# mLSTM cell and leaky-ReLU feed-forward: cells in fewer groups, k, v and x asked for by ScalarE, and three float32r products in groups 4 and 5

## The chip, the cores and the metric

The kernel runs on one core of a Trainium2 chip. Times are device microseconds (us) of one execution. Shown for the kernel before are the median of three runs, 513.25 us (510.64 to 513.26), and one profiled execution. PE is TensorE, PEld its weight loads, DVE VectorE, ACT ScalarE, POOL GpSimd, SP SyncE.

## The reference

An mLSTM cell runs over a sequence; its output, rearranged to one row of 320 values per token, passes a two-layer feed-forward with a leaky ReLU:

```python
batch, n_heads, seq, head_dim = (4, 8, 768, 40)          # d_model 320, d_ff 2048
for t in range(S):
    m_new = np.maximum(f_gate[:, :, t] + m, i_gate[:, :, t])
    f_stab = np.exp(f_gate[:, :, t] + m - m_new)
    i_stab = np.exp(i_gate[:, :, t] - m_new)
    C = f_stab[:, :, None, None] * C + i_stab[:, :, None, None] * np.einsum('bhd,bhe->bhde', vt, kt)
    n = f_stab[:, :, None] * n + i_stab[:, :, None] * kt
    h_tilde = np.einsum('bhde,bhe->bhd', C, qt)
    denom = np.maximum(np.abs(np.einsum('bhd,bhd->bh', n, qt)[:, :, None]), 1.0)
    y[:, :, t] = h_tilde / denom / (1.0 + np.exp(-o_gate[:, :, t]))
...
x = y.transpose(0, 2, 1, 3).reshape(B * S, H * D)         # 3072 x 320
h = x @ w_in                                              # 320 x 2048
out = np.maximum(0.01 * h, h) @ w_out                     # 2048 x 320
```

All of it is float32 (the two weight matrices arrive as 64-bit words and are made float32 on the chip).

## The kernel before, in words

**Chunks, steps, groups.** The sequence is cut into NB = 6 chunks c of 128 tokens. A cell step s = 4c + b is one chunk of one of the four batches. The four steps of chunk c make x of group c: 512 tokens, on which the feed-forward then works. So cells of a later chunk run beside the feed-forward of an earlier group.

**The first product** of a group (`ff_units`, its matmul on line 759) makes 2048 hidden columns in 16 blocks f of 128, two blocks to a pair j, one on each half of the partitions (row group r). The 320 rows of the contraction are five slots of 64; for each slot there is one matmul per row group, with 64 rows of weights and 512 tokens of x. A pair is two units: three slots, then two slots and two Prelus on ACT (line 767), which take the two PSUM banks `ph` to the tile `acts`. These banks are two of the four in the pool `psf`; the cells have four of their own in `psc`.

**The second product** of groups 1 to 5 (`fast_units`) goes by seven block products in place of eight, each for two batches n: 14 units, in the order p1, p2, p6, p7, p4, p5, p3, each of 16 matmuls of 160 columns (line 835) into one bank of `psf`. Sums on DVE (lines 853, 858, 862, 870, 887, 892; `mix_early`, line 822), copies on ACT (854, 867, 875, 881) and sums on POOL (868, 876, 882) empty these banks or make operands; line 848 sends rows out through SP. Group 0 has a plain second product (line 794). A group of 1 to 5 thus has 30 units: 16 and 14.

**The cells** of chunks 2 to 5 come in pairs of steps. `u_parts` (scores on lines 614 and 619, DVE on 596 and 624) and `u_mix` (matmuls on line 695, transposes on DVE on lines 702 and 713, POOL on 709, four writes of x to DRAM on line 716 by SP) are a step's two units. `ahead(s)` prepares a later step: exponentials on ACT (458), transposed k and q on DVE (505, 511), the state on POOL (592). `prep_mask` (450) is POOL's. `feed` asks for a step's data: `load`, with k on line 356 and four pieces of v on line 359, and `spread`, line 413; `load_blocks` fetches q, k and o in blocks (398), `spread_q` (421) gate rows. `gather_x` (line 730) reads x back from DRAM in the layout of the first product, four DMAs a step. All these DMAs are on SP.

**The order.** PE, DVE, ACT and POOL run in the order in which the program is written (`manual_schedule`); SP's DMAs are placed by the scheduler. A last loop, lines 1043 to 1103, writes the order: for chunk c it goes through the 30 units of group c - 1 and lays chunk c's cell units behind the unit numbers in `place` (chunk 1) or `pairs` (chunks 2 to 5):

```python
pairs = (2, 2, 6, 6, 14, 14, 19, 19, 19)
```

So chunk 5's cells run beside group 4, and group 5 runs alone. In a unit's place come, in order: steps of exponentials, masks at units 0 and 12, the unit itself, cell units, gathers (from unit 15 on, all steps that are mixed), `ahead`, and `feed`.

**Memory.** Cell tiles (k and q operands, S, rb, w, kqT and others) lie in pools that stay open to the end: `consts` and `wk`. DMAs use eight semaphores in turn, whichever engine asks; a DMA waits for the eighth before it.

Of the kernel before, what the change touches and what calls it, by code (L numbers as in the profile page):

```python
# [10 lines left out]
U32 = mybir.dt.uint32  # L11
U64 = mybir.dt.uint64
# [6 lines left out]
def kernel(  # L19
# [58 lines left out]
    dr = ctx.enter_context(tc.tile_pool(name="dr", bufs=1, space=bass.MemoryType.DRAM))  # L78

# [39 lines left out]
    kn = consts.tile([P, NL, H, DP], F32, name="kn")  # L119
    qn = consts.tile([P, NL, H, DP], F32, name="qn")  # L120
    S_t = [consts.tile([P, 2, H, DP], F32, name=f"S{n}") for n in range(NL)]
    S_v = [t[:].rearrange("p u h (k d) -> p u h k d", d=QW) for t in S_t]
    rb_t = [consts.tile([P, 3, RW], F32, name=f"rb{n}") for n in range(NR)]
    xb = consts.tile([P, PR * TB, QW], F32, name="xb")
# [147 lines left out]
    def gates(c):  # L272


        m0 = m0s.get(c)
        n = P if c == 0 else BH
        fc, il = (f0[:], i0[:]) if c == 0 else (fi[c][:, 0, :], fi[c][:, 1, :])
        F = wk.tile([n, P], F32, name="F", bufs=1)
        nc.vector.tensor_tensor_scan(F[:], fc, zeros[:n].to_broadcast([n, P]), 0.0, op0=ALU.add, op1=ALU.add)
        if c > 0:  # L280
            il_t = wk.tile([BH, P], F32, name="il", bufs=1)
            nc.vector.tensor_scalar(il_t[:], il, scalar1=m0[:], scalar2=None, op0=ALU.subtract)
            il = il_t[:]
        m = wk.tile([n, P], F32, name="m", bufs=1)
        nc.vector.tensor_tensor_scan(m[:], fc, il, -1e30 if c == 0 else 0.0, op0=ALU.add, op1=ALU.max)
        a = wk.tile([n, P], F32, name="a", bufs=1)
        nc.vector.tensor_tensor(a[:], F[:], m[:], op=ALU.subtract)
        bu = wk.tile([BH, 3, P], F32, name="bu", bufs=1)
        nc.vector.tensor_tensor(bu[:, 0, :], il[:BH], F[:BH], op=ALU.subtract)
        if c + 1 < NB:  # L290
            m1 = wk.tile([BH, 1], F32, name="m0")
            if c == 0:
                nc.vector.tensor_copy(m1[:], m[:BH, P - 1 :])
            else:
                nc.vector.tensor_tensor(m1[:], m0[:], m[:, P - 1 :], op=ALU.add)
            m0s[c + 1] = m1
        if c > 0:
            na = wk.tile([BH, 1], F32, name="na")
            nc.vector.tensor_tensor(na[:], m[:, SL - 1 : SL], F[:, SL - 1 : SL], op=ALU.subtract)
        bus[c] = bu, a, (na if c > 0 else None)  # L300
# [42 lines left out]

    def load(s):
        c, b = divmod(s, B)
        rows = ts(c, P)
        d = st.setdefault(s, {})
        n = s % NL
        d.update(k=kn[:, n], q=qn[:, n])
        if c == 0:  # L350
            d["va"] = S_t[n][:, 1]
            parts = [(d["k"][:, :, :D], k), (d["q"][:, :, :D], q), (d["va"][:, :, :D], v)]
            for dst, src in parts:
                nc.sync.dma_start(dst, src[b, :, rows, :].rearrange("h p d -> p h d"))
            return
        nc.sync.dma_start(d["k"][:, :, :D], k[b, :, rows, :].rearrange("h p d -> p h d"))
        for u in range(2):
            for i in range(2):
                nc.sync.dma_start(  # L359
                    S_v[n][ts(u, SL), u, :, i, :DB],  # L360
                    v[b, :, c * P + u * SL : c * P + (u + 1) * SL, DB * i : DB * (i + 1)].rearrange("h p d -> p h d"),
                )
# [43 lines left out]
    def spread(s):  # L406

        c, b = divmod(s, B)
        d = st[s]
        w = wk.tile([P, H, P], F32, name="w", bufs=NL)  # L410
        d["w"] = w[:].rearrange("p h t -> p (h t)")[:, : H * SL].rearrange("p (h t) -> p h t", t=SL)
        for u in range(2):
            nc.sync.dma_start(d["w"][ts(u, SL)], a_dr[c, 0, u, b * H : (b + 1) * H, :].partition_broadcast(SL))

    def spread_q(s):

        c, b = divmod(s, B)
        d = st.setdefault(s, {})
        d["ea"] = wk.tile([P, H, SL], F32, name="ea", bufs=EAB)
        for r in range(2):  # L420
            nc.sync.dma_start(
                d["ea"][ts(r, SL)], a_dr[c, 1, 1 - r, b * H : (b + 1) * H, :].partition_broadcast(SL),
            )

    def spread_first(a, s2):
# [12 lines left out]
        for n in range(2):  # L438
            w = st[s2 + n]["w"] = wk.tile([P, H, P], F32, name="w", bufs=NL)
# [20 lines left out]
    def prep_vu(s):  # L460
# [3 lines left out]
        if s < NS:  # L464
            d["vu"] = wk.tile([P, H, 2, V1], F32, name="vu")
# [34 lines left out]
    def prep_kq(s):  # L500

        d = st[s]
        d["kqT"] = wk.tile([P, 2, PR * P], F32, name="kqT")
# [20 lines left out]
    def u_split(s):  # L524

        d = st[s]
        d["kqT"] = wk.tile([P, 2, PR * P], F32, name="kqT")
# [14 lines left out]
    def u_transpose(s):  # L542
        d = st[s]
        d["kqT"] = wk.tile([P, 2, PR * P], F32, name="kqT")
# [92 lines left out]
    def u_values(s):  # L637
# [4 lines left out]
        d["den"] = wk.tile([P, H], F32, name="den")  # L642
        denominators(d["den"][:], pa[:, :, D])

    def gate(s):

        d = st[s]
        d["x"] = wk.tile([P, Dm], F32, name="x")
# [7 lines left out]
    def u_plain(s):  # L656
# [13 lines left out]
        den = wk.tile([P, H], F32, name="den")  # L670
        denominators(den[:], hN[:, :, 0, DB])
        if b < 2:
            d["x"] = wk.tile([P, Dm], F32, name="x")[:]
        else:
            d["x"] = wk.tile([P, H, D1], F32, name="hn")[:].rearrange("p h d -> p (h d)")[:, :Dm]
# [8 lines left out]
    def u_mix(s):  # L684
# [16 lines left out]
        hb = wk.tile([P, PR * TB, QW], F32, name="hb", bufs=1)  # L701
        nc.vector.transpose(hb[:].rearrange("p (j n) d -> p j n d", n=TB), in_blocks(pT[:]))  # L702
        den = wk.tile([P, PR * TB], F32, name="den")
# [8 lines left out]
        xq = wk.tile([P, PR * P], F32, name="x")  # L712
# [6 lines left out]
    def gather_x(s):  # L719

        c, b = divmod(s, B)
        if ("xT", c) not in st:
            st["xT", c] = wk.tile([P, KC, GT], F32, name="xT", bufs=1)
        xT = st["xT", c]
        src = x_dr[s].rearrange("(k p) t -> p k t", p=DP)
        for r in range(2):
            at = 0
            while at < KC:
                k0, n = run_of(r, at)
                nc.sync.dma_start(xT[DP * r : DP * (r + 1), at : at + n, ts(b, P)], src[:, k0 : k0 + 2 * n - 1 : 2, :])  # L730
                at += n

# [20 lines left out]
    def ff_units(g):  # L753
        xT = st["xT", g]
# [59 lines left out]
        return firsts + fast_units(g)  # L814
# [104 lines left out]
    def ahead(s):  # L919

        if s < NS:
            if s < 2 * B:
                u_split(s)
# [98 lines left out]
    with tc.manual_schedule(engines={E.PE, E.DVE, E.Activation, E.Pool}):  # L1022
# [20 lines left out]
        for c in range(1, NB + 1):  # L1043
            if c > 1:
                ffs = ff_units(c - 1)
            cells = cell_units(c) if c < NB else []
            n_ff, n_c = len(ffs), len(cells)
            done = fed = 0
            waiting, after = [], []
            for i in range(n_ff):  # L1050
                if c == 1:
                    run(now, 2 if i < 10 else 3 if i < 14 else 4)
                    for n in fetch.get(i, ()):
                        load_weights(QN + n)
                    if i == 0:
                        prep_mask(B)
                        ahead(B)
                        load_fi(3)
                for s, steps in lazy.items():
                    if s in late and late[s] > 0:  # L1060
                        late[s] -= 1
                    else:
                        run(steps, 3)
                for n in masks.get(i, ()) if 1 < c < NB else ():
                    if c * B + n < NS:
                        prep_mask(c * B + n)
                ffs[i]()
                if c + 1 < NB:
                    if i == (1 if c == 1 else 0):
                        gates(c + 1)  # L1070
                    if c == 2 and i == 0:
                        mixed_weights()
                    if i == (3 if c == 1 else 2):
                        gates_exp(c + 1)
                upto = min(n_c, sum(p <= i for p in (place if c == 1 else pairs)))
                while done < upto:
                    fn, s = cells[done]
                    fn(s)
                    done += 1
                    if fn is u_mix:  # L1080
                        waiting.append(s)
                    if fn is u_plain and s < 2 * B - 1 or fn is u_parts and s == 2 * B - 1:
                        ahead(s + 1)
                    elif fn is u_mix:
                        after.append(s + 2)
                    elif fn is u_plain:
                        prep_mask(s + 2)
                        ahead(s + 2)
                if i >= NF - 1:
                    for s in waiting:  # L1090
                        gather_x(s)
                    waiting.clear()
                if i < NF or i >= NF + 8:
                    for s in after:
                        ahead(s)
                    after.clear()
                while fed < done:
                    fn, s = cells[fed]
                    fed += 1
                    if fn in (u_mix, u_plain):  # L1100
                        load_late(s + NR, 2)
                        if s + NL < NS:
                            feed(s + NL)
# [31 lines left out]
```

## Time and profile before

| | us |
|---|---|
| median of the runs shown (lowest, highest) | 513.25 (510.64, 513.26) |
| span of the profiled execution, first to last instruction (no other time is given for it) | 508.0 |
| PE, DVE, ACT, POOL busy | 492.0, 308.1, 171.5, 137.7 |
| mean granted TensorE clock | 0.983 |
| PE starts groups 1, 2, 3, 4, 5 at | 139.3, 214.1, 289.0, 365.3, 439.7 |
| first product of group 5, 439.7 to | 474.3 |

An engine's busy time says how much work it has, not that it sets the end. That is read from the chain that ended last (from the last instruction back to what released each step), and then, stage by stage, from the idle time of the engine that stands in the chain. A row of a group gives line, engine, operation, `out<-in` tiles, count, busy time and mean time of one, then the idle time just before it and what ended most of it.

### The profile page before, as it was taken

The page shows a single profiled execution, that of the slowest core. Times are in us where ns is not written, and L with a number is a line of the kernel's source. Part 1 is how long each engine was busy: PE and PEld are TensorE (multiplying, and loading weights), DVE is VectorE, ACT ScalarE, POOL GpSimd, SP SyncE. Part 2 cuts the span into 40 slices and gives each one's busy share as a digit, 9 for nine tenths or more (in the row PEclk, how much of TensorE's full clock was granted, in tenths as well). Part 3 has the DMA queues.
Part 4 walks back from the last instruction along what each step waited for, and adds up shares of the span by engine and source line. Part 5 has one row for each costly group of instructions (what it writes and reads, how often), then busy time and mean ns, then how long its engine had stood idle before and what let it go on. Part 6 is the DMA issues. An engine that isn't in the chain of part 4 may idle for free.

```text
span 508.0 us, 12526 instructions
## 1 busy us (share of the span) xinstructions
PE 492.0 (97%) x4981; PEld 366.6 (72%) x4981; DVE 308.1 (61%) x515; ACT 171.5 (34%) x478; POOL 137.7 (27%) x175
## 2 busy tenths in 40 slices
PE   8878999999999999999999999999899999999997
PEld 7766878767655489955589855599755599744797
DVE  4779898899954778635765826764825664101321
ACT  3664864652722510323411323311213411022210
POOL 4243443360402404413104614014612003000020
PEclk9877999999999999999999999999999999999999
DMA  9977687888765551565663566564466212200001
GB/s 116 146 204 154 149 219 185 168 152 175 155 145 87 131 124 46 133 130 144 147 132 92 115 137 170 137 141 97 109 135 177 68 53 62 69 1 1 1 1 52
DMA packets 165290, 59.21 MB, mean 117 GB/s; under 512 B 128816, under 2 KB 156016, under 8 KB 165232
## 3 DMA queue, kind: packets, MB, share of 16 engines
q1 hardware_dynamic: 164848, 58.28, 52.2%
q8 instruction: 39, 0.64, 0.5%
q14 instruction: 19, 0.16, 0.1%
q10 hardware_dynamic: 384, 0.13, 0.1%
HBM read 51.68 MB, written 6.70 MB: 115 GB/s over the span
## 4 chain that ended last, share of the span: by engine, by line
PE 79%; DVE 9%; DMA 3%; ACT 3%; POOL 2%; issue 2%; SPq 2%; ACTq 0%; POOLq 0%; DVEq 0%
PE ph L759 36%; PE po L835 26%; PE po L794 6%; PE pT L695 3%; PE sd L614 3%; SPq L359 1%; PE sd L619 1%; DMA S<-in_v_dram 1%; ACT kqT L540 1%; PE tkq L548 1%; DVE raw L261 1%; DMA rb<-in_q_dram 1%; DMA w<-a_dr 1%; PE pa L641 1%; DVE qn L511 1%
## 5 line engine op out<-in xcount | busy, mean ns | idle before, releaser
L759 PE MATMUL ph<-xT,w_in 64*128 64x512 f32 (+1 forms) x1120 | 216.2, 538 | 2.4 <-DVE y L887 1.4
L759 PEld LDWEIGHTS ph<-xT,w_in 64*128 64x128 f32 x1120 | 108.6, 189 | 95.1 <-issue 86.3
L767 ACT ACTIVATE acts<-ph 128x512 f32<-128x512 f32 (+1 forms) x112 | 53.9, 533 | 179.0 <-PE ph L759 178.9
L835 PEld LDWEIGHTS po<-w_out,acts 128*128 128x128 f32 x640 | 87.3, 190 | 3.8 <-issue 3.8
L835 PE MATMUL po<-w_out,acts 128*128 128x160 f32 x640 | 89.1, 300 | 0.0
L450 POOL TENSOR_TENSOR w<-w,i 128x512 f32<-128x512 f32 x20 | 26.9, 1345 | 117.3 <-DMA w<-a_dr 117.2
L624 DVE TENSOR_TENSOR qn<-w,sd 64x512 f32<-64x512 f32 x40 | 27.4, 684 | 40.2 <-PE sd L619 20.5
L458 ACT ACTIVATE w<-w,gT 128x64 f32<-128x64 f32 (+1 forms) x192 | 50.8, 348 | 2.7 <-POOL w L450 1.7
L592 POOL TENSOR_TENSOR S<-S,f 40x336 f32<-40x336 f32 x36 | 32.0, 889 | 67.3 <-PE pT L695 36.3
L835 PE MATMUL po<-raw,acts 128*128 128x160 f32 x320 | 45.5, 300 | 0.0
L835 PEld LDWEIGHTS po<-raw,acts 128*128 128x128 f32 x320 | 43.9, 190 | 0.3
L794 PE MATMUL po<-w_out,acts 128*128 128x320 f32 x128 | 36.5, 436 | 0.0
L702 DVE STREAM_TRANSPOSE hb<-pT 128x512 f32<-128x512 f32 x16 | 11.5, 717 | 31.0 <-PE pT L695 30.8
L794 PEld LDWEIGHTS po<-w_out,acts 128*128 128x128 f32 x128 | 23.6, 190 | 9.3 <-issue 0.3
L511 DVE TENSOR_TENSOR qn<-kqT,ea 64x512 f32<-64x512 f32 x32 | 28.4, 888 | 1.0
L709 POOL TENSOR_TENSOR xb<-xb,den 128x320 f32<-128x320 f32 x16 | 11.7, 729 | 56.8 <-DVE xb L706 56.6
L596 DVE TENSOR_TENSOR S<-S,sd 40x336 f32<-40x336 f32 x36 | 18.1, 503 | 12.1 <-POOL S L592 11.2
L614 PEld LDWEIGHTS sd<-kqT 40*64 40x64 f32 x640 | 19.9, 135 | 6.1 <-issue 6.1
L822 DVE TENSOR_TENSOR raw<-acts 128x1024 f32<-128x1024 f32 x10 | 11.8, 1222 | 18.3 <-ACT acts L767 18.2
L713 DVE STREAM_TRANSPOSE x<-xb 128x512 f32<-128x512 f32 x16 | 18.2, 1140 | 7.6 <-POOL xb L709 7.6
L835 PE MATMUL po<-raw 128*128 128x160 f32 x160 | 22.5, 299 | 0.0
L835 PEld LDWEIGHTS po<-raw 128*128 128x128 f32 x160 | 22.0, 190 | 0.0
(151 smaller groups left out, 551.8 us busy)
## 6 DMA issues: line engine op xcount, KB each, us to landing
w<-a_dr SPq DMA_DIRECT2D x40, 128.0 KB
rb<-in_k_dram SPq DMA_DIRECT2D x64, 80.0 KB
rb<-in_q_dram SPq DMA_DIRECT2D x64, 80.0 KB
rb<-in_o_gate_dram SPq DMA_DIRECT2D x64, 80.0 KB
ea<-a_dr SPq DMA_DIRECT2D x32, 128.0 KB
kn<-in_k_dram SPq DMA_DIRECT2D x24, 160.0 KB
raw<-in_moe_w_out_dram SPq DMA_DIRECT2D x6, 640.0 KB
S<-in_v_dram SPq DMA_DIRECT2D x80, 40.0 KB
```

The costliest lines, as they stand in the source:

```text
L450: nc.gpsimd.tensor_tensor(w, w, cm2.unsqueeze(1).to_broadcast([P, H, SL]), op=ALU.add)
L458: yield nc.scalar.activation(w[:, h, :], w[:, h, :], AF.Exp, bias=gT[c][:, 0, bh : bh + 1], scale=1.0)
L511: nc.vector.tensor_tensor(mixed(s)[rows, 1 - r], d["kqT"][rows, 1].rearrange("p (h t) -> p h t", t=SL), d["ea"][rows], op=ALU.mult,)
L592: nc.gpsimd.tensor_tensor(new, old, g, op=ALU.mult)
L596: nc.vector.tensor_tensor(new, new, st[s]["dC", u], op=ALU.add)
L614: nc.tensor.matmul(bank[1 - u][toks, h, :], lhsT=kqT[rows, 0, ts(h, SL)], rhs=kqT[rows, 1, ts(h, SL)], start=True, stop=True,)
L624: nc.vector.tensor_tensor(mixed(s)[toks, u], w[toks], bank[1 - u][toks], op=ALU.mult)
L713: nc.vector.transpose(in_blocks(xq[:]), xb[:].rearrange("p (j n) d -> p j n d", n=TB))
L759: nc.tensor.matmul(ph[r][:, cols], lhsT=w_row(r, slot, j), rhs=xT[DP * r : DP * (r + 1), slot, cols], start=(slot == 0), stop=(slot == KC ...
L767: nc.scalar.activation(acts[:, f, cols], ph[r][:, cols], AF.Prelu, alpha=0.01)
L794: nc.tensor.matmul(po[n][:], lhsT=acts[:, f, ts(n, P)], rhs=w_out[:, f, :], start=(f == 0), stop=(f == NF - 1),)
L835: nc.tensor.matmul(bank[:], lhsT=left[:, f, :], rhs=right[:, f, :], start=f == 0, stop=f == KH - 1)
```

## The change

It has three parts.

- **Pace.** Ticks take the place of unit numbers: after i + 1 units of group g, the cells stand at tick (30(g - 1) + i + 1) * 4 // 3. Chunk 2's cells still start with group 1, and chunk 5's end at unit 22 of group 3 (tick ENDS = 109) in place of unit 19 of group 4. Order within a tick is as before. At ENDS the cell pools `cc` and `cw`, into which the cell tiles have moved, are closed, and a pool `kp` takes their memory.
- **Asked for by ScalarE.** From chunk 3 on, `load` makes a generator of five DMAs, which ACT issues from two units later on: one a unit in a first product, two in a second. `gather_x` is issued by ACT too, one step a unit, at least three units after the step's `u_mix`. The queue of SP keeps the rest.
- **Three products.** In groups 4 and 5 (in group 4 without its first two pairs, LEAD = 2) the first product of a slot becomes three with float32r operands: raw by raw and low by low into `ph`, dif by dif into a bank `pe` of `psc`. `low` and `dif` of weights and x are made by `split_w_parts` (masking on DVE, difference on POOL, a sum on DVE, a scaled copy on ACT, for each half of 640 columns) and `split_x` (three on DVE for a batch). `raw` weights are copied within SBUF by SP (`fetch_w_part`). `prepare` runs these steps from ENDS on, three a unit in a first product and two in a second; x of group 5 is split in units 4 to 10 of group 4's second product.

```diff
-                nc.sync.dma_start(xT[DP * r : DP * (r + 1), at : at + n, ts(b, P)], src[:, k0 : k0 + 2 * n - 1 : 2, :])
+                nc.scalar.dma_start(xT[DP * r : DP * (r + 1), at : at + n, ts(b, P)], src[:, k0 : k0 + 2 * n - 1 : 2, :])
...
+        if c < 3:
+            for _ in bring(nc.sync):
+                pass
+        else:
+            later[s] = [bring(nc.scalar), 5, clock[0] + 2]
...
+    EPS = 2.0**-12
+    THREE = (NB - 2, NB - 1)
...
+        def first():
+            t = tmp_part()[:].rearrange("p k t -> p (k t)")
+            held.append(t)
+            top_bits(t, src)
+            nc.gpsimd.tensor_tensor(t, t, src, op=ALU.subtract)
+
+        def second():
+            t = held[0]
+            nc.vector.scalar_tensor_tensor(
+                parts["w", "dif"][n][:, at], in0=t, scalar=1.0 + 1.0 / EPS, in1=src, op0=ALU.mult, op1=ALU.add,
+            )
+            nc.scalar.activation(parts["w", "low"][n][:, at], t, AF.Copy, scale=1.0 / EPS)
...
+            def first():
+                ph.extend(psf.tile([P, GT], F32, name=f"ph{r}", tag="mm") for r in range(2))
+                rows(j, ph, "raw", True, False)
+
+            def second():
+                rows(j, ph, "low", False, True)
+
+            def third():
+                pe.extend(psc.tile([P, GT], F32, name=f"pe{r}", tag="c") for r in range(2))
+                rows(j, pe, "dif", True, True)
+                fs = [acts[:, f_of(r, j), :] for r in range(2)]
+                for r in range(2):
+                    nc.scalar.activation(fs[r], pe[r][:], AF.Copy, scale=-EPS)
+                for r in range(2):
+                    nc.vector.scalar_tensor_tensor(
+                        fs[r], in0=ph[r][:], scalar=1.0 + EPS, in1=fs[r], op0=ALU.mult, op1=ALU.add,
+                    )
+                for r in range(2):
+                    nc.scalar.activation(fs[r], fs[r], AF.Prelu, alpha=0.01)
...
+            for i in range(len(ffs)):
+                at["past"] = i >= len(firsts) - 1
+                upto = min(ENDS + 1, (TICKS * (g - 1) + i + 1) * 4 // 3)
+                for m in range(t, upto):
+                    before_tick(m)
                 ffs[i]()
...
+                for m in range(t, upto):
+                    after_tick(m)
+                gather()
+                if t <= ENDS < upto:
+                    open_parts()
+                    for n in range(QN):
+                        fetch_w_part(n)
+                    todo = split_steps()
+                t = max(t, upto)
+                clock[0] += 1
+                bring_later(1 if i < len(firsts) else 2)
+                prepare(3 if i < len(firsts) else 2)
```

## The prediction

> **What bounds the kernel now.** I read the busy times first, then the chain that ended last, then the engines' busy time by stage. The first lines are from the page; the next from the busy time by stretches, cut at the starts of groups 1, 2, 3, 4 and 5 (columns: stretch, its length, busy time and count of PE, PEld, DVE, ACT, POOL, then the granted clock, DMA share, GB/s).
>
> ```profile
> PE 492.0 (97%) x4981; PEld 366.6 (72%) x4981; DVE 308.1 (61%) x515; ACT 171.5 (34%) x478; POOL 137.7 (27%) x175
> ...
> PE ph L759 36%; PE po L835 26%; PE po L794 6%; PE pT L695 3%; PE sd L614 3%; SPq L359 1%; PE sd L619 1%; DMA S<-in_v_dram 1%; ACT kqT L540 1%; PE tkq L548 1%; DVE raw L261 1%; DMA rb<-in_q_dram 1%; DMA w<-a_dr 1%; PE pa L641 1%; DVE qn L511 1%
> ```
> ```profile
> 139.30:214.10 74.80, 74.80 (x775) 54.15 (x774) 49.35 (x76) 21.45 (x65) 21.27 (x25) 1.00 0.49 109
> 214.10:289.00 74.90, 74.90 (x776) 54.17 (x775) 46.08 (x81) 21.05 (x64) 24.07 (x26) 1.00 0.56 129
> 289.00:365.20 76.20, 74.86 (x775) 54.15 (x774) 46.42 (x78) 21.14 (x64) 23.56 (x26) 1.00 0.58 130
> 365.20:439.70 74.50, 74.44 (x704) 54.03 (x704) 36.74 (x64) 16.26 (x44) 12.17 (x16) 1.00 0.41 100
> 439.70:508.00 68.30, 65.25 (x385) 45.86 (x384) 11.98 (x17) 11.03 (x24) 3.14 (x6) 1.00 0.04 13
> ```
>
> The reader is to see that from 139 us on PE has no idle time but 1.4 us ahead of group 4 and the tail, at full granted clock. So only two things change the time there: matmul work, and new waits of PE. Group 5, without cells, costs 65.2 us: 34.6 for the first product (439.7 to 474.3) and 30.7 for the second; a cell chunk adds 9.6 us of PE to groups 1 to 4.
>
> Two more views carry the prices: PE's and PEld's order of time in a first product, PE's waits, and the DMA issues on SP (min/median/max ns).
>
> ```profile
> 236.66 0.19 PEld L759 LDWEIGHTS ph<-xT,w_in 64*128 64x128 f32 x2 [0.23 <-issue]
> 237.09 0.19 PEld L759 LDWEIGHTS ph<-xT,w_in 64*128 64x128 f32 x2 [0.23 <-issue]
> ```
> ```profile
> PE ph L759 <- DVE y L887: 1.4, 1, 1.4
> ```
> ```profile
> L730 SPq DMA_DIRECT2D xT<-x_dr x64: 573/607/1462, 184.9 to 431.6; - x64
> ```
> ```profile
> L359 SPq DMA_DIRECT2D S<-in_v_dram x80: 595/630/2971, 41.9 to 374.6; - x80
> ```
>
> One float32 product of 512 columns is two instructions on each of two row groups (line 759's row counts 1120: 800 for the 400 products of groups 1 to 5, 320 for the 160 of 256 columns in group 0). The row groups run side by side: two loads appear together every 0.43 us. So a pair of products costs 2 x 0.43; over group 5, 34.6 / 40 = 0.865 us.
>
> **The change part by part.**
>
> *Three float32r products.* Six of eight column pairs in group 4 and all eight in group 5, five slots each: 70 pairs of products lose 0.865 us and get three float32r pairs. No row shows a float32r matmul. Bounds: it is at least the shortest spacing of weight loads, 0.11 us (line 641: sixteen in 1.98 us, the last taking 0.28), and I bound it above by one float32 instruction, 0.428 us. That is 70 x (0.33 - 0.865) = -37 us to 70 x (1.284 - 0.865) = +29 us. I take the middle by ratio, 0.214, half a float32 instruction: the row nearest in kind streams the same 512 columns with a split operand. Three cost 0.642; the gain is 70 x 0.223 = **15.6 us**.
>
> The Trainium skill (FP8 and Floating Point Precision, TensorE Precision Notes) says that true FP32 takes four passes and that reduced-precision FP32 is read as four bytes and truncated. One pass would be an estimated 0.216 us by it, the gain 15.1 us; no run shows it yet.
>
> *Epilogue of a triple.* Per column pair ACT gains two copies (0.59 each, line 767) beside its two Prelus, DVE two sums (0.68, line 564). After a third unit PE's bank is free 0.6 + 0.7 + 0.7 = 2.0 us later; PE takes 15 x 0.214 = 3.2 us for the next triple in the other banks. Hidden; if DVE is over 1.2 us behind, it shows.
>
> *Splitting the weights and x.* Per half of 640 columns: DVE 0.49 (line 253) + 0.83 (257), ACT 0.79 (247), POOL 1.1 to 1.6 (from 0.53 at 160 and 0.73 at 320 columns, and from 1.27 at 512 in line 450); I take 1.3, near the first. A batch of x: 0.49 + 0.83 + 0.83 = 2.15 us of DVE. In total 16 x 1.32 + 8 x 2.15 = 38 us of DVE. Group 5's x hides under group 4's second product (DVE busy 12 us in a group without cells). The rest is queued on DVE right behind the last cells, in units 22 to 29 of group 3, and there it is not hidden. Queue it by hand, with t = 0 where PE ends the last cell product. In the trace before, DVE ended that cell's transpose 6.6 us after such an end (417.9 to 424.5). The first masking operation must wait until both last cells' x are in DRAM, since its tile takes their memory: four issues of 0.34 us on SP and 1.4 us to land (from the semaphore times around 164 us): t = 9.7. From there, in program order: three maskings and three differences, waiting for POOL and ACT, to 15.4; x of batch 0 to 17.5; the sums that free bank 1 (the former line 887) 18.1; batch 1 and a masking 20.8; sums freeing bank 2 at 21.4; a difference and batch 2 at 24.3; line 892's sum 24.6; batch 3, a masking, the other sum at 27.6. PE meanwhile: seven units of 2.24 us. The third-last product waits for an ACT copy that stands behind the first new ACT operation: 12.9 in place of 11.2. Group 4's first pair wants both banks: 21.4 in place of 15.7. Its second pair wants the last sum: 27.7 to 32.0, against 24.3 without waits. **7.7 us**, plus 1 for DVE operations that stretch beside POOL (line 511: median 0.73, max 1.54); the 1.4 us of today is in it. Net +7.3. By the time of the first triple, 32 us, every part it needs is made.
>
> *Cells at 4/3.* PE's sum is unchanged; groups 1 to 3 become 65.2 + 4/3 x 9.6 = 78 us. DVE: 12 for the products + 4/3 x 35 = 59 of 78. Enough on average. Where its queue shows: in group 1 the second cell pair's operands (6.0 us in the trace) stand ahead of the second p2 sum, which frees a bank: +1.2 us by the same queue. At unit 27 of group 1 a cell pair and the next pair's operands (7.0 + 6.0 us) stand ahead of the last sums, so group 2's second and third column pair take the banks that the Prelu just before gives back: 1.3 + 0.7 = +2.0 us. Groups 2 and 3 end otherwise: 0.
>
> *Loads asked for by ACT.* 60 loads of k and v (0.43 and 0.63 us) and 64 gathers (0.61): 72 us leave SP's queue and enter ACT's, over 235 us in which ACT is 28% busy; with cells at 4/3 it comes to some 50 of 78 us in a group. What stands behind an issue on ACT are exponentials, Prelus and copies that free banks. A Prelu pair is due 4.3 us after its products and takes 1.2, so 3.1 us of delay cost nothing. I cost it at 0; below zero it can't be, as PE was not idle for SP. It brings one more wait: eight semaphores are shared by both queues, and every DMA waits for the eighth before it in program order, whichever engine asked.
>
> Sum: -15.6 + 7.3 + 1.2 + 2.0 = -5.1 us. The span of 508.0 becomes 502.9. The median shown is 513.25, 5.25 above that span (the lowest run is 2.6 above); I keep the 5.25: **508 us**.
>
> **Rivals.**
> - *The seams are covered*: DVE reaches the parts earlier or banks fall otherwise. For: group ends today cost 0, 0 and 1.4. Then 513.25 - 15.6 + 0 to 5 = 498 to 503.
> - *ACT waits behind SP* (slower). SP waited 29.8 us for DVE at the x writes (line 716), longest 8.6. If an ACT load inherits such a wait by the shared semaphores once in groups 1, 2 and 3, each costs 8.6 - 3.1 = 5.5 us: 508 + 16.5 = 524.5. It decides where ACT stands over 3.1 us in a first product. Against: the loads are delayed by two units, so by over 4 us.
> - *float32r runs at a float32 instruction's pace* (the change doesn't do what it says): 508 + 15.6 + 29 = 553.
> - *Weight loads come out of hiding*: if a load could not run under a matmul of its own row group, a float32r product cost 0.214 + 0.113 = 0.327, three 0.98: +8.1 in place of -15.6, 532 us. The trace speaks against: float32 instructions start 0.43 us apart with 0.19 of load inside.
>
> The Trainium skill (TensorE: Matmul & The Clock Gate, Part 3) says that loads overlap running matmuls only where the row group differs; by that float32 would already show 0.113 more, which the trace does not.
>
> - *In between*: float32r near 0.24 us, or a few more waits: 511 to 516.
>
> **How the numbers follow.** Forecast (503 to 512.5) 0.45; covered seams 0.20; in between 0.07; ACT 0.17; exposed loads 0.04; slow float32r 0.07. 0.5%, about what a measurement of this kernel can tell from no change, is 2.6 us: faster is below 510.7. Of the forecast's 0.45 some 0.35 lie there and 0.10 within. Faster 0.55; same 0.10 + 0.07 + 0.01 = 0.18; slower 0.27. The range reaches from the covered seams to ACT's rival, 497 to 525, and leaves the last two out.
>
> **What would show it.** float32r rows of line 839 of the changed kernel: starts 0.21 us apart for a pair (right), 0.33 or 0.43 (wrong). The first product of group 5 near 26 us in place of 34.6. PE's waits: the first float32 pairs of group 4 on DVE, 6 to 9 us together; about 2 on ACT early in group 2. ACT's waits on DMA over 3 us in groups 1 to 3 would make it wrong, as would PE idle within the triples.

## The result and the profile after

The changed kernel takes 546.57 us (544.56 to 547.68, four runs), the kernel before 511.94 us (509.50 to 513.26) in the same comparison: ratio 1.069, 95% interval 1.064 to 1.073. It is slower, by 35 us, and outside the range that was given. Its profiled execution took 547.39 us with a span of 545.6. One execution of the kernel at 6/5 below took 708 us at a granted clock of 0.65 and is left out of its time.

The page of the changed kernel, engines and chain of work:

```profile
PE 495.0 (91%) x5121; PEld 390.7 (72%) x5121; DVE 361.3 (66%) x583; ACT 194.6 (36%) x514; POOL 154.4 (28%) x183
...
PE 55%; DMA 11%; DVE 11%; SPq 10%; issue 3%; POOL 3%; ACTq 3%; ACT 3%; DVEq 0%; POOLq 0%
```

PE has gone from 97% to 91% of a longer span, and from 79% to 55% of the chain; the chain now runs through DMAs, DVE and SP's queue. Busy time by stretches, cut at the starts of groups 1 to 5 of the changed kernel (columns as before):

```profile
140.30:224.73 84.43, 79.99 (x967) 58.05 (x966) 58.48 (x105) 25.70 (x83) 27.02 (x30) 1.00 0.58 123
224.73:333.64 108.91, 84.31 (x973) 62.95 (x972) 60.91 (x107) 23.26 (x70) 30.02 (x34) 0.91 0.64 145
333.64:414.94 81.30, 76.61 (x707) 55.42 (x705) 56.33 (x85) 22.78 (x64) 27.89 (x27) 0.97 0.43 107
414.94:483.92 68.98, 64.86 (x446) 53.63 (x446) 45.77 (x61) 21.15 (x40) 11.44 (x10) 0.95 0.12 37
483.92:545.60 61.68, 58.51 (x465) 52.83 (x464) 22.10 (x33) 20.76 (x40) 3.13 (x6) 1.00 0.04 14
```

| us | before | after | difference | PE's waits, before and after |
|---|---|---|---|---|
| to the start of group 1 | 139.3 | 140.3 | +1.0 | |
| group 1 | 74.8 | 84.4 | +9.6 | 0 and 4.4 |
| group 2 | 74.9 | 108.9 | +34.0 | 0 and 24.6 |
| group 3 | 76.3 | 81.3 | +5.0 | 1.4 and 4.7 |
| group 4 | 74.5 | 69.0 | -5.5 | 0 and 4.1 |
| group 5 and tail | 68.3 | 61.7 | -6.6 | 0 and 0 |

Groups 1 and 2 hold the cells of one and a half chunks each (1.5 x 9.6 = 14.4 us, 4.8 more than before), group 3 of one, group 4 of none: that sums to nothing. What is left of the 37.6 us of span: PE's waits from group 1 on, 37.9 in place of 1.4, **+36.5**; clock lost behind these waits (PE's busy time by single microseconds, times one less the granted clock; nothing before), **+7.4**; the triples, **-12.2**; the time ahead of group 1, +1.0 (among the profiled runs of this study group 1 began anywhere from 135.9 to 142.0); and +4.9 left in PE's busy time, which I did not take apart. By the same sums some 2.3 us of it lie in group 2 and 2.2 in group 4. Group 4 has no cells, so cell and block products that lie mixed more closely can't be the whole of it; where the experiments leave group 4 without waits, it has no such rest.

PE's longest waits in the changed kernel (who waits, for whom: us in all, times, longest):

```profile
PE tg L332 <- DVE S L630: 19.0, 1, 19.0
PE ph L902 <- DVE y L1030: 5.0, 2, 2.8
PE po L978 <- DVE acts L1001: 2.8, 2, 2.1
PE po L978 <- ACT y L1010: 2.8, 1, 2.8
PE ph L902 <- ACT acts L910: 2.2, 3, 1.3
```

One wait makes half of it. Lines of the changed kernel: 902 is the first product (759 before), 978 the block product (835), 484 the mask (450), 1025 and 1030 the last sums of p4 on POOL and of p5 on DVE (882, 887). Who else waits between 290 and 340 us tells what the 19 us hang on:

```profile
POOL w L484 <- DMA w<-a_dr: 22.5, 2, 20.3
...
DVE hn L1030 <- POOL hn L1025: 21.2, 1, 21.2
...
PE tg L332 <- DVE S L630: 19.0, 1, 19.0
```

Read from the bottom: PE's gate transposes wait for DVE's state update; that stands on DVE behind p5's sum, which waits for p4's sum on POOL; that stands on POOL behind the mask of steps 20 and 21, which waits for gate rows w that SP has not brought. POOL's order of time in the changed kernel, and SP's issues that it waits for (the first of two w at 316.81):

```profile
299.17 1.00 POOL L1019 TENSOR_TENSOR hn<-hn,y 128x160 f32<-128x160 f32 x2
320.46 1.26 POOL L484 TENSOR_TENSOR w<-w,i 128x512 f32<-128x512 f32 x1 [20.29 <-DMA w<-a_dr]
323.90 1.26 POOL L484 TENSOR_TENSOR w<-w,i 128x512 f32<-128x512 f32 x1 [2.18 <-DMA w<-a_dr]
325.12 1.00 POOL L1025 TENSOR_TENSOR hn<-hn 128x160 f32<-128x160 f32 x2
```

```profile
314.76 1.95 SPq L432 DMA_DIRECT2D rb<-in_o_gate_dram  x4
316.81 1.09 SPq L447 DMA_DIRECT2D w<-a_dr  x2
```

And the same mask in the trace of the kernel before, on POOL:

```profile
341.37 1.27 POOL L450 TENSOR_TENSOR w<-w,i 128x512 f32<-128x512 f32 x1 [22.95 <-DMA w<-a_dr]
```

This is the line to learn from: POOL waited as long for the same rows before, 22.95 us. It cost PE little, because the mask stood at unit 12 of group 3, in the program ahead of the whole second product: POOL had done both masks by 349.0 and the last sum of p4 by 364.1, where PE came to group 4 at 363.9. At 4/3 of the pace tick 12 of that chunk is unit 24 of group 2, where the mask stands ahead of both sums of p4.

It was not quite free before either. DVE waited 6.23 us for a state update that stands on POOL behind the second mask, and had no gap over 0.4 us from there to the sums of line 887, which PE waited 1.4 us for, its only wait:

```profile
349.85 0.51 DVE L596 TENSOR_TENSOR S<-S,sd 40x336 f32<-40x336 f32 x1 [6.23 <-POOL S L592]
```

The triples can be read from PE's order of time in group 5 of the changed kernel (x10 is five slots on two row groups):

```profile
485.19 1.32 PE L839 MATMUL ph<-x_low,w_low 64*128 64x512 f32 x10
486.34 1.30 PE L839 MATMUL pe<-x_dif,w_dif 64*128 64x512 f32 x10
487.47 1.33 PE L839 MATMUL ph<-xT,w_raw 64*128 64x512 f32 x10
488.64 1.32 PE L839 MATMUL ph<-x_low,w_low 64*128 64x512 f32 x10
```

From one low product to the next are 3.45 us: 0.230 us for a pair of row groups, against 0.865 with float32.

### The profile page after: what moved, and what is told of

Read it like the earlier page. It is cut to its first block, busy times and chain, and to the rows that moved or that the text cites. A ratio compares the mean times of both kernels' runs of the same rounds, so it can differ in the third digit from the quotient of the medians.

```text
span 545.6 us, 12928 instructions
## 1 busy us (share of the span) xinstructions
PE 495.0 (91%) x5121; PEld 390.7 (72%) x5121; DVE 361.3 (66%) x583; ACT 194.6 (36%) x514; POOL 154.4 (28%) x183
## 4 chain that ended last, share of the span: by engine, by line
PE 55%; DMA 11%; DVE 11%; SPq 10%; issue 3%; POOL 3%; ACTq 3%; ACT 3%; DVEq 0%; POOLq 0%
PE po L978 17%; PE ph L902 13%; PE ph L839 6%; PE po L937 5%; SPq L432 4%; PE pe L839 3%; DMA kn<-in_k_dram 2%; PE pT L729 2%; DMA rb<-in_o_gate_dram 2%; DMA rb<-in_k_dram 2%; PE pa L675 2%; PE sd L648 2%; SPq L386 2%; ACTq L764 1%; DMA S<-in_v_dram 1%
## 5 line engine op out<-in xcount | busy, mean ns | idle before, releaser
L902 PE MATMUL ph<-xT,w_in 64*128 64x512 f32 (+1 forms) x840 | 159.5, 526 | 7.6 <-DVE y L1030 5.0
L902 PEld LDWEIGHTS ph<-xT,w_in 64*128 64x128 f32 x840 | 83.9, 192 | 72.3 <-issue 55.2
L978 PE MATMUL po<-w_out,acts 128*128 128x160 f32 x640 | 92.1, 304 | 1.9 <-ACT hn L1024 1.9
L978 PEld LDWEIGHTS po<-w_out,acts 128*128 128x128 f32 x640 | 89.1, 193 | 5.3 <-issue 3.0
L910 ACT ACTIVATE acts<-ph 128x512 f32<-128x512 f32 (+1 forms) x84 | 38.6, 512 | 94.6 <-PE ph L902 93.7
L484 POOL TENSOR_TENSOR w<-w,i 128x512 f32<-128x512 f32 x20 | 28.9, 1450 | 64.0 <-DMA w<-a_dr 61.9
L1011 POOL TENSOR_TENSOR y<-y,raw 128x160 f32<-128x160 f32 x10 | 8.0, 806 | 120.7 <-ACT y L1010 120.7
L861 DVE SCALAR_TENSOR_TENSOR acts<-ph,acts 128x512 f32<-128x512 f32 x28 | 18.0, 686 | 28.1 <-ACT acts L859 28.1
L937 PE MATMUL po<-w_out,acts 128*128 128x320 f32 x128 | 36.5, 436 | 0.0
L1030 DVE TENSOR_TENSOR hn<-hn,po 128x160 f32<-128x160 f32 x10 | 3.2, 317 | 42.0 <-POOL hn L1025 21.2
L937 PEld LDWEIGHTS po<-w_out,acts 128*128 128x128 f32 x128 | 23.6, 190 | 9.3 <-issue 0.3
L743 POOL TENSOR_TENSOR xb<-xb,den 128x320 f32<-128x320 f32 x16 | 11.7, 728 | 53.0 <-DVE xb L740 53.0
L859 ACT ACTIVATE acts<-pe 128x512 f32<-128x512 f32 x28 | 15.2, 596 | 23.6 <-PE pe L839 23.6
```

Source lines behind the costliest of these rows:

```text
L484: nc.gpsimd.tensor_tensor(w, w, cm2.unsqueeze(1).to_broadcast([P, H, SL]), op=ALU.add)
L902: nc.tensor.matmul(ph[r][:, cols], lhsT=w_row(r, slot, j), rhs=xT[DP * r : DP * (r + 1), slot, cols], start=(slot == 0), stop=(slot == KC ...
L910: nc.scalar.activation(acts[:, f, cols], ph[r][:, cols], AF.Prelu, alpha=0.01)
L937: nc.tensor.matmul(po[n][:], lhsT=acts[:, f, ts(n, P)], rhs=w_out[:, f, :], start=(f == 0), stop=(f == NF - 1),)
L978: nc.tensor.matmul(bank[:], lhsT=left[:, f, :], rhs=right[:, f, :], start=f == 0, stop=f == KH - 1)
```

## The experiments

"Waits" are PE's from group 1 on, by profile. Each kernel starts from the changed one unless it says otherwise; ratios are to the kernel before, in runs on the same chip.

**Masks four ticks later.**

```diff
-        masks = {0: (2, 3), 12: (4, 5)}
+        masks = {0: (2, 3), 16: (4, 5)}
```

> The changed kernel with the two later masks of a chunk written at tick 16 in place of tick 12, so that POOL's masks of steps 20 and 21 stand behind the last POOL sums of group 2 and not ahead of them. Theory 'mask' (POOL waits for w of chunk 5, and the sums of p4 that PE's banks need stand behind it): the 19 us wait of PE at the end of group 2 goes, and most of the low clock after it; 546.6 - 19 - 3 = 523 to 527 us. Rival 'w is late for everyone' (SP brings w at 320 us whatever POOL does, and ACT's exponentials of steps 20 and 21, which stand ahead of Prelus, wait for it instead): part of the wait comes back at the start of group 3; 530 to 540 us. Rival 'gate transposes' (the wait of PE is the state update's own): no change, 543 to 550 us.

Measured: 528.57 us, ratio 1.038 (1.033 to 1.043): 18 us less by the medians, 16 by the ratios. The profiled runs, from the start of group 1 to PE's end, differ by 13.8 us: group 2 is 21.6 shorter, group 3 is 5.0 and groups 1 and 4 together 2.8 longer. What is left lies ahead of group 1 (136.0 us in place of 140.3), where this edit changes nothing. POOL's sums now end at 298 and the 19 us are gone. But the time lies above the 523 to 527 of the mask alone, since the rival is true as well: SP still brings its rows at 316 to 320, and ACT meets them next. PE's and ACT's waits from 300 to 330 us of this kernel:

```profile
PE ph L902 <- ACT acts L910: 3.2, 1, 3.2
```

```profile
ACT rb L528 <- DMA rb<-in_o_gate_dram: 22.9, 2, 19.8
```

ACT's activation of the o gates (line 528) stands ahead of group 3's first Prelus and waits 19.8 us for its rows, also asked for by SP; PE gets 3.2 us of that. So the mask's place is the cause of the 19 us, and what made it dear is a late SP.

**All loads and gathers by SP**, at the same places.

```diff
-            later[s] = [bring(nc.scalar), 5, clock[0] + 2]
+            later[s] = [bring(nc.sync), 5, clock[0] + 2]
...
-                nc.scalar.dma_start(xT[DP * r : DP * (r + 1), at : at + n, ts(b, P)], src[:, k0 : k0 + 2 * n - 1 : 2, :])
+                nc.sync.dma_start(xT[DP * r : DP * (r + 1), at : at + n, ts(b, P)], src[:, k0 : k0 + 2 * n - 1 : 2, :])
```

> The changed kernel with the loads of k and v and the gathers of x issued by SP, at the same places of the program. Theory 'shared semaphores' (SP stood for 20 us of group 2 waiting for DMAs that ACT had yet to issue, and so brought w of chunk 5 late): w lands 9 to 15 us earlier, PE's wait at the end of group 2 falls from 19 to 4 to 10 us, ACT's waits for DMAs (2.8 and 2.1 us of PE in groups 1 and 2) go: 528 to 537 us. Theory 'pace alone' (w is late since ten ticks are now seven and a half units, and SP has to issue 72 us more): 543 to 552 us.

Measured: 549.6 us, ratio 1.078 (1.073 to 1.083). w does not come 9 to 15 us earlier: its first issue on SP is at 317.72 in place of 316.81. Whether ACT's issues held up SP in the changed kernel (by its profile SP waited 20 us for DMAs of ACT between 225 and 335 us) the run doesn't show: those waits are gone, but SP now has these issues to make itself, and makes them one behind the other from 285 us on. POOL's and PE's waits from 280 to 340 us of this kernel:

```profile
POOL w L484 <- DMA w<-a_dr: 31.0, 2, 28.9
...
PE tg L332 <- DVE S L630: 25.5, 1, 25.5
```

PE's wait of 2.8 us for a copy on ACT in group 1 is gone, as expected; 4.7 us for gathered x at the start of group 2 stand in its place.

**No triples, nothing split** (`THREE = ()`).

```diff
-    THREE = (NB - 2, NB - 1)
+    THREE = ()
...
```

> The changed kernel without the three products: groups 4 and 5 with float32 matmuls, nothing split. By the rows of the changed kernel a triple is 3.45 us in place of 4.33, 14 of them 12.3 us, and the seam between groups 3 and 4 costs 8.8 us of PE waits and some 3 of low clock. So group 5's first product goes from 27.9 back to 34.6 us, the seam falls to 0 to 2 us, the wait at the end of group 2 stays at 19: 544 to 549 us if both are right. If the seam is not the splitting (but the cells' pace), it stays and the time is 556 to 560 us.

Measured: 541.04 us, ratio 1.065 (1.057 to 1.072), a little under what was expected. The 18.6 us at the end of group 2 stay, the seam between groups 3 and 4 has no wait at all, and groups 4 and 5 take 65.2 us each. From the start of group 3 to PE's end the changed kernel takes 208.8 us, this one 204.4: the triples' 12.2 us and more were spent on the splitting in the changed kernel.

**Splitting from group 4's first unit**, with five float32 pairs ahead.

```diff
-        LEAD = 2
+        LEAD = 5
...
-                prepare(3 if i < len(firsts) else 2)
+                if g > 3:
+                    prepare(3 if i < len(firsts) else 2)
```

> The changed kernel with the splitting begun at group 4's first unit in place of unit 22 of group 3, and five float32 pairs ahead of the triples in place of two. Theory 'seam' (DVE's splitting stands ahead of the sums that free the banks): PE's waits of 8.8 us around the start of group 4 and the low clock behind them go, three pairs more in float32 cost 3 x 0.88 = 2.6 us: 535 to 540 us. Rival (the splitting is only moved, and the Prelus, copies and the first triples wait for it): 543 to 549 us.

Measured: 542.02 us, ratio 1.064 (1.060 to 1.068). The seam's waits go, as the theory said (0 in place of 7.3 us around the start of group 4), and one of 6.5 us comes at the first triple: the rival in part. Its x is ready (the last sum for it ends at 425.8). What it waits for is a bank: the first of the Prelus that free it ends at 434.49, and these stand on ACT behind scaled copies `w_low`, each of which waits for POOL's difference. PE's and ACT's order of time in this kernel:

```profile
434.59 1.66 PE L839 MATMUL ph<-xT,w_raw 64*128 64x512 f32 x5 [6.46 <-issue]
```

```profile
430.80 0.74 ACT L812 ACTIVATE w_low<-tmp 128x640 fp32r<-128x640 f32 x1 [1.74 <-POOL tmp L805]
433.27 0.74 ACT L812 ACTIVATE w_low<-tmp 128x640 fp32r<-128x640 f32 x1 [1.73 <-POOL tmp L805]
433.91 2.04 ACT L910 ACTIVATE acts<-ph 128x512 f32<-128x512 f32 x4
```

**The pace of before**, with ACT's issues, and triples in group 5 only after three float32 pairs; the splitting of what these need runs a step a unit from unit 19 of group 4.

```diff
-    THREE = (NB - 2, NB - 1)
+    THREE = (NB - 1,)
...
-        LEAD = 2
+        LEAD = 3
...
-                upto = min(ENDS + 1, (TICKS * (g - 1) + i + 1) * 4 // 3)
+                upto = min(ENDS + 1, (TICKS * (g - 1) + i + 1) * 1 // 1)
...
-                prepare(3 if i < len(firsts) else 2)
+                prepare(2 if g in THREE else 1)
```

> The changed kernel with one tick a unit, the pace of before: chunk 5's cells end at unit 19 of group 4, only group 5 has the three products, with three float32 pairs ahead; the loads of k and v and the gathers stay with ACT. Theory 'pace' (the tick of the masks falls among POOL's sums at 4/3 only): no wait of PE over 2 us at a group's end; the gain is 5 triples x 0.88 = 4.4 us, the splitting of half the weights costs 0 to 2 at the start of group 5: 4.4 to 2 us under the kernel before of the same runs, 0.991 to 0.996 of it. Theory 'ACT' (waits of ACT at its DMA issues delay copies and Prelus at any pace): two to four waits of 2 to 3 us in groups 1 to 4, and the low clock behind them: 1.00 to 1.02.

Measured: 504.61 us, ratio 0.991 (0.988 to 0.994), as 'pace' had it. Groups 1 to 3 have no wait, the clock is 1.00 from 139 us on. Group 5 takes 61.1 us to PE's end; group 4 76.5, with 1.7 us of waits for ACT copies that stand behind splitting. Whether the triples or ACT's issues bring the gain this run can't tell; the one with the issues alone, below, can.

**The same with loads and gathers by SP.**

> The same as the one before it, with the loads of k and v and the gathers issued by SP. If ACT's issues cost nothing at the old pace, the two agree within 2 us. If ACT's waits cost PE time, this one is 3 to 8 us the faster: 0.985 to 0.996 of the kernel before. If SP is the narrower queue (25 us of PE's wait in place of 19 when SP had all the loads at 4/3), this one is slower by 1 to 5 us.

Measured: 524.3 us, ratio 1.029 (1.023 to 1.035), worse than any of the expectations. PE waits 3.2, 2.5 and 3.4 us for gathered x at the starts of groups 2, 3 and 4: at their later places these DMAs stand in a full queue (SP's issues follow each other from 195 to 220 us with no gap over 0.2 us, gathers for group 2 among them).

**Three waits moved away at 4/3**: masks at tick 16, exponentials five units later, splitting from group 4's first unit, first of what its four triples need.

```diff
-                late[s] = 3
+                late[s] = 8
...
-        masks = {0: (2, 3), 12: (4, 5)}
+        masks = {0: (2, 3), 16: (4, 5)}
...
-        LEAD = 2
+        LEAD = 4
...
-            halves = [(n, half) for n in range(QN) for half in range(2)]
+            halves = [(n % QN, half) for n in range(LEAD // 2, LEAD // 2 + QN) for half in range(2)]
...
-                prepare(3 if i < len(firsts) else 2)
+                if g > 3:
+                    prepare(3 if i < 4 else 0 if i < len(firsts) else 1)
```

> The changed kernel at 4/3 with three waits moved away: the later masks at tick 16, the exponentials of a step five units later (which in the run with the masks alone stood ahead of Prelus, 3.2 us of PE), and the splitting from group 4's first unit on, first of what its four triples need (four float32 pairs ahead of them). From 528.6 us with the masks alone: less 3.2 for the Prelus, less some 6 for the seam and some 5 of low clock, plus 2 x 0.88 for two pairs more: 514 to 518 us. What is left over the kernel before is then waits in groups 1 and 2 (9 us), less 10.5 for twelve triples, and 5 for cells that lie closer. Rival (the waits move on to the next in line on DVE or ACT): 521 to 530 us.

Measured: 524.14 us, ratio 1.027 (1.022 to 1.033): the rival. Group 4 is now what the triples make it (61.8 us, 65.2 less four times 0.88), but groups 1 to 3 keep 15.2 us of waits, and 4.5 us of clock behind them. The longest, 4.3 us at the start of group 3, has the cause that was met before: ACT's activation of the o gates waits 17.1 us for its rows. The longest in group 2 shows ACT's issues at work. ACT's order of time in this kernel:

```profile
278.76 2.56 ACTq L764 DMA_DIRECT2D xT<-x_dr  x4
281.36 1.31 ACTq L386 DMA_DIRECT2D S<-in_v_dram  x2
282.71 0.29 ACT L997 COPY raw<-po 128x160 f32<-128x160 f32 x1 [4.83 <-DMA xT<-x_dr]
...
283.78 1.28 ACT L492 ACTIVATE w<-w,gT 128x64 f32<-128x64 f32 x5
```

Gathers and loads hold ACT from 278.76 to 282.67; a copy and the exponentials of line 492 stand behind them, DVE waits 3.5 us for these, and PE 4.2 us for DVE's state update.

**6/5 in place of 4/3**, the splitting much as in the last kernel; masks and exponentials stand at the ticks of the changed kernel.

```diff
-                upto = min(ENDS + 1, (TICKS * (g - 1) + i + 1) * 4 // 3)
+                upto = min(ENDS + 1, (TICKS * (g - 1) + i + 1) * 6 // 5)
...
```

> The changed kernel at 6/5 in place of 4/3: chunk 5's cells end at unit 1 of group 4, the masks of chunk 5 fall behind POOL's sums of group 2 by themselves, the splitting runs from there as in the run ahead of this one, with four float32 pairs in group 4. Twelve triples gain 12 x 0.88 = 10.5 us. If POOL's masks among the sums and DVE's splitting were the whole cost of the pace, waits are 2 to 6 us: 502 to 508 us, 0.985 to 0.995 of the kernel before. If a faster pace always sets cell work against the sums that free the banks: 512 to 520 us.

Measured: 534.76 us (five executions), ratio 1.046 (1.038 to 1.054), slower than at 4/3 with three waits moved. The whole difference lies in group 4: 79.8 us in place of 61.8, with 9.3 us of waits and 5.7 of low clock, where PE waits for Prelus that stand on ACT behind the splitting (4.4 and 5.0 us). Groups 1 to 3 take 253.1 us in place of 256.1, with some 2 us less of cells; waits and low clock in them come to 21.5 us in place of 19.7. So the time does not show what the pace alone costs. DVE's order of time ahead of a wait of 7.4 us in group 2 (line 1000 is line 1001 of the changed kernel):

```profile
265.48 0.51 DVE L630 TENSOR_TENSOR S<-S,sd 40x336 f32<-40x336 f32 x1 [7.30 <-POOL S L626]
...
272.48 1.88 DVE L545 TENSOR_TENSOR qn<-kqT,ea 64x512 f32<-64x512 f32 x2
274.39 1.31 DVE L539 STREAM_TRANSPOSE kqT<-rb 128x512 f32<-128x512 f32 x2
275.73 1.39 DVE L545 TENSOR_TENSOR qn<-kqT,ea 64x512 f32<-64x512 f32 x2
277.14 3.31 DVE L995 TENSOR_TENSOR acts<-acts 128x1024 f32<-128x1024 f32 x2
280.38 2.35 DVE L1000 TENSOR_TENSOR acts<-acts 128x1024 f32<-128x1024 f32 x2
```

Two steps' k and q operands (`ahead`) stand right before the sums that are the next products' operands, and DVE is late for them from 265.48 on, where it has waited 7.30 us for a state update on POOL. That update stands behind masks that waited 22.2 us for w. The 2.1 us for line 1001 in the changed kernel's waits come the same way: DVE has no gap over 0.4 us between 260.44, where it has waited 5.80 us for POOL behind a mask that waited 25.4 us for w, and these sums.

**ACT's issues alone**, at the pace of before, without triples.

> One tick a unit and no three products anywhere: of the change, the loads of k and v and the gathers issued by ACT are left, each at its later place. If they cost nothing and bring nothing at this pace, the time is that of the kernel before within 0.5%, with group 4 at 74 to 75 us and group 5 at 65.2. If the gain of the run at the old pace (0.991) came from these issues and not from the triples, it is 0.99 here too. If they cost, 1.01.

Measured: 505.97 us, ratio 0.993 (0.990 to 0.996). They gain, and most of what the run at the old pace gained. By stages from group 1 to PE's end it is 363.6 in place of 365.6 us: the 1.4 us ahead of group 4 and 0.5 in group 4 go. The masks find their rows here: where POOL waited 22.95 us for them before, it does not wait at all:

```profile
318.82 2.96 POOL L484 TENSOR_TENSOR w<-w,i 128x512 f32<-128x512 f32 x2
```

So at the old pace w was late because SP asked for k, v and x as well. The rest of the 0.7% lies ahead of group 1 or in the runs' scatter; I could not place it.

**Splitting later at the old pace**, from unit 25 of group 4 on, four float32 pairs.

```diff
...
-        LEAD = 2
+        LEAD = 4
...
-                prepare(3 if i < len(firsts) else 2)
+                if g in THREE or i >= 25:
+                    prepare(2 if g in THREE else 1)
```

> One tick a unit, the three products in group 5 only, with four float32 pairs ahead and the splitting begun at unit 25 of group 4, behind the copies and sums that free the banks, in place of unit 19. In the run at the old pace group 4's second product took 35.4 us, 2.5 more than before, as ACT's and POOL's splitting stood ahead of copies. Theory: those 2.5 us go, one pair more costs 0.88; group 4 at 74.5, group 5 at 61.7 us, 3.5 us under the kernel before and 1.5 under the run at the old pace: 0.990 to 0.994 of before, against 0.991. Rival (the splitting is then late for the first triple): a wait of 2 to 5 us in group 5, 0.997 to 1.003.

Measured: 503.19 us, ratio 0.987 (0.983 to 0.991): the best of all, faster than both kernels. PE has no wait from 139 us to its end. Groups 4 and 5 of this kernel:

```profile
361.70:435.70 74.00, 74.00 (x705) 53.41 (x704) 40.36 (x64) 17.64 (x46) 14.33 (x18) 1.00 0.35 104
435.70:500.80 65.10, 61.89 (x425) 49.63 (x424) 29.36 (x41) 17.21 (x34) 5.79 (x8) 0.99 0.04 13
```

PE is busy for all of group 4, and group 5's PE time is 61.9 in place of 65.2: four triples, each 0.83 shorter. By stages from group 1 to PE's end that is 5.4 us under the kernel before, of which ACT's issues alone bring 2.1 and the triples the rest.

**Gathers by ACT, loads by SP**, otherwise the run at the old pace.

> The run at the old pace (0.991 of before) with the loads of k and v issued by SP and the gathers by ACT. With both on SP, PE waited 3.2, 2.5 and 3.4 us for gathered x at the starts of groups 2, 3 and 4, and the time was 1.029 of before. If gathers late in SP's queue were the whole of it, this one agrees with the run at the old pace: 0.988 to 0.995. If the loads on SP hold up what the gathers wait for (x's writes), it is 1.01 to 1.03.

Measured: 508.10 us, ratio 0.996 (0.993 to 0.999), between the two expectations. PE's waits for gathered x are gone, and with them most of the 20 us that SP cost at this pace. The loads account for the smaller part; with them on SP the masks wait for w again, 23.2 us at the longest. Gathers by SP with the loads left to ACT were not run.

## Why the prediction was wrong

**The step that failed** is "Groups 2 and 3 end otherwise: 0". For groups 1 and 3 I queued DVE by hand; for group 2 I looked at DVE alone and never at what POOL has between its sums. The mask was in the trace of before with a wait of 22.95 us, and the tick arithmetic puts it ahead of p4's sums. It cost 19 us of waiting and 2.4 of clock in group 2: moving it took 21.6 us off group 2, and 14 to 18 off the whole, as a late SP took a part back in group 3.

**Low clock behind waits** is missing from every sum: 7.4 us in the changed kernel.

**ACT's issues.** "I cost it at 0": in group 1 a copy behind them cost PE 2.8 us. It is not the rival's mechanism, which had ACT inherit a wait of SP in a first product. The longest wait of ACT ahead of such a copy, 11.7 us, holds fourteen issues, and they alone take 10.6 us of it:

```profile
194.77 3.15 ACTq L764 DMA_DIRECT2D xT<-x_dr  x4
...
199.71 3.30 ACTq L764 DMA_DIRECT2D xT<-x_dr  x4
...
206.72 0.29 ACT L1010 COPY y<-po 128x160 f32<-128x160 f32 x1 [11.68 <-DMA xT<-x_dr]
```

The prediction priced a delay by what a Prelu pair of a first product can bear, 3.1 us. In a second product two loads and the four DMAs of a gather can stand in one unit of 2.24 us, at some 0.6 us each. With the issues on SP this wait of PE is gone.

"Below zero it can't be, as PE was not idle for SP" was wrong too: at the old pace these issues are worth 0.7%, 2 us of it seen by stages. PE's 1.4 us ahead of group 4 were a wait for SP, at one remove: w, the mask on POOL, DVE's state update, DVE's sum.

**The float32r products** were mis-sized a little: 0.230 us a pair in place of 0.214, a gain of 70 x (0.865 - 0.690) = 12.2 us in place of 15.6. The rivals with 0.327 and 0.428 fall. By the Trainium skill's note on passes (FP8 and Floating Point Precision, TensorE Precision Notes) the prediction had estimated 0.216; the trace has 0.230, nearly the one pass.

**The seam of groups 3 and 4** was right in kind: waits of 1.9, 2.8, 2.2 and 0.4 us, 7.3 in all, at the places where 8.7 were worked out by hand. A fifth, 1.5 us at the first triple, was held to be nothing: there a Prelu stands on ACT behind a scaled copy that waits for POOL, so it is luck that the sum, 8.8, fits so well. The runs without triples and with the splitting moved show that it is the splitting. The low clock behind it, 4.4 us, was not counted.

**Group 1**: the p2 sum was given 1.2 us and took 0.9 (line 1005). **Group 2's first pairs**: 2.0 given, 0.7 measured.

**Cells at 4/3** do not spread evenly: groups 1 and 2 hold one and a half chunks, group 3 one. The 78 us that the prediction gave each of these groups held for none. DVE was busy 58.5 and 60.9 us in groups 1 and 2, near the 59 that the average gave; that it had time enough did not keep its sums from coming late.

**The base.** I added 5.25 us to the span. The profiled run of the changed kernel took 1.8 us more than its span (547.39 and 545.6), so some 3.4 us of the forecast were the choice of the base.

Of the 35 us, then, the mask with its clock is settled by experiment, the seam and ACT's copy too; DVE's operand sums in groups 1 and 2 are read from the traces, and the 4.9 us in PE's busy time stay open. Why SP brings w some 20 us after the mask's place is shown for the old pace: with k, v and x asked for by ACT the wait is gone. In the changed kernel they are asked for by ACT and w is late all the same; there it stays open. SP's issues go back to back from 304 to 320 us, in the order in which the scheduler put them.

## What to carry to other kernels

An engine that waits long and harmlessly is a debt: before work is moved to another pace, list each engine's longest waits (POOL's too) and look what would be queued behind each at its new place. An engine's average load says little here: the same cell work cost 1.4 us of waits at the old places and, with three waits already moved away, still 15 us of waits and 4.5 of clock at the new ones. And a saving on the bound engine (12 us of triples) is worth what its preparation leaves of it; with four triples and the splitting put behind the last sums it paid, 0.987 of before, where ACT's issues alone gave 0.993.

## What the hardware showed

A short wait of PE can cost nearly twice its length: 1.9 us at 404 were followed by 3.4 us at half clock, 1.7 us of work lost. Stretches of the changed kernel behind its longest wait and in the seam (the granted clock is the third figure from the right):

```profile
328.00:331.00 3.00, 2.21 (x24) 2.14 (x26) 2.96 (x10) 0.00 (x0) 0.00 (x0) 0.50 0.42 107
331.00:334.00 3.00, 3.00 (x54) 2.88 (x52) 1.90 (x7) 0.00 (x0) 0.76 (x1) 0.50 0.76 234
...
418.00:421.00 3.00, 2.75 (x8) 1.21 (x10) 2.96 (x4) 0.74 (x1) 1.35 (x1) 0.50 0.15 55
421.00:424.00 3.00, 3.00 (x11) 1.21 (x8) 2.93 (x5) 0.00 (x0) 0.00 (x0) 0.57 0.13 49
```

After the 19 us the clock stayed at half for 6 us of further work; after waits of 2.8 and 2.2 us it was half from 417 to 424. One of 2.8 us at 204 did not bring it, while one of 2.5 us at the same place did in the run with the later masks. In all thirteen traces the stretches at half clock are whole multiples of 3.41 us long (3.41, 6.83 and 20.48 us in this one), but for the last of each, which the end of the trace cuts off. The Trainium skill (TensorE: Matmul & The Clock Gate, Part 1) says that the clock falls to half after an idle window of about 3.4 us that runs freely, and comes back after as much busy time. The halves agree, and so does the chance in it; the waits that were enough here are shorter than that window.
